# Attention scores: the second product of each block made over 128 rows instead of 68

## The chip, the cores and the metric

The kernel runs on one core of one Trainium2 chip. A core has TensorE (PE: matrix products; PEld is its loading of weights), VectorE (DVE), ScalarE (ACT), GpSimd (POOL) and SyncE (SP, which here issues most transfers). The metric is the device time of one execution in microseconds (us). [...]

## What is computed

Attention with a causal mask and a bias that falls with the distance, then a layer of eight experts of which each row takes one, then a mixing layer. Only the first part is touched:

```python
scores = scale * np.matmul(q, k.transpose(0, 1, 3, 2))        # 4 x 8 heads, 576 x 576, head size 64
cum = np.cumsum(np.maximum(s, 0.0), axis=-1)
bias = -(cum[:, :, :, None] - cum[:, :, None, :])
scores = np.where(causal, -1e9, scores + np.minimum(bias, 0.0))
attn = np.exp(scores - max); attn = attn / (attn.sum() + 1e-9)
out = np.matmul(attn, v)
# then the experts (w_gate, w_local, w1, w2) and the mixing layer (U, V, w_ch1, w_ch2)
```

## The kernel before

The program is written out by hand for each engine: `ORDER` (lines 29 to 127) is a list of numbers that says in which order the pieces of the attention, of the router and of the first expert's work are issued, and each engine works through its own list in that order.

The 32 heads are taken in 16 pairs. For each pair the kernel builds a stack `OP` of 128 rows (two buffers, used in turn, line 416). Its columns are four blocks of 576: K1, Q1, K2, Q2. Each of q and k is split into a high and a low part, so that a product of the two is a sum of three products. The first 64 rows of K1 and Q1, and the last 64, together hold two of them, and the **first product** (lines 725 to 731) contracts all 128 rows of Q1 with K1. K2 and Q2 hold the third in rows 0 to 63, and in rows 64 to 67 the two parts of the bias (cumulated sums against ones), so the **second product** (lines 732 to 738) contracts rows 0 to 67 (`SK = D + 4`) and adds to the same place. Rows 68 to 127 of K2 and Q2 aren't used. In a block on the diagonal a third, small product with a 128x128 mask follows (line 740).

A pair has five blocks of rows (`t` = 0 to 4), each with two parts; so there are 16 x 6 x 2 = 192 first and 192 second products, with 64 to 448 columns. After a block's products DVE takes the largest of each row (line 749), ACT the exponentials (line 766), PE turns them (line 795), ACT and DVE split them (lines 803 and 808), and PE multiplies them with v (line 844).

The stack is filled by transfers on SP's queue: `bias(n)` writes rows 64 to 67 of K2 and Q2 (lines 461 to 465) and `stack` copies the parts (line 557). For the first pair ACT, DVE and POOL write the parts themselves (`split_twice`, lines 1299 to 1318), POOL the block Q2 (line 1304). Of the setup code the prediction speaks of the reading of `s` and its cumulated sum on DVE (lines 424 to 437), and of the loads of `v` that POOL issues (line 1323).

## Time and profile before

| | us |
|---|---|
| runs, median of 3 | 997.5 (996.58 to 1003.1) |
| the profiled execution, its own time | 1002.29 |
| its span, from the first instruction to the last | 1000.6 |
| PE busy in the span | 946.6 |
| DVE, ACT, POOL busy | 550.6, 455.1, 235.2 |

The span is what the profile shows; the time of the same execution is 1.7 us more. Attention and routing take about the first 300 us, the experts and the mixing layer the rest. The mean granted clock over the span is 0.969.

### The profile page before, as it was taken

Reading aid. Unit: us, or ns where it says so; the run is one execution under the profiler, and the core shown is the slowest. Engines: PE = TensorE matmul, PEld = TensorE weight load, DVE = VectorE, ACT = ScalarE, POOL = GpSimd, SP = SyncE. Lnnn points to the kernel's source line nnn. Section 1 sums busy time; section 2 is a strip of 40 time slices with the busy share of each in tenths; the row PEclk is TensorE's granted clock in tenths of the full one; section 3 lists DMA queues with packets and bytes.
Section 4 is the critical chain, followed back from the end, with each engine's and each line's share of the span. In section 5 each row is a group of like instructions: output and inputs, shape, how many; then the busy total and the mean of one; then the engine's idle time right before and its main releaser. Section 6 shows DMA issues by size and latency. Waiting matters only on the chain.

```text
span 1000.6 us, 17314 instructions
## 1 busy us (share of the span) xinstructions
PE 946.6 (95%) x6378; PEld 727.8 (73%) x6378; DVE 550.6 (55%) x1168; ACT 455.1 (45%) x1040; POOL 235.2 (24%) x355
## 2 busy tenths in 40 slices
PE   5888988989899899999999999999999999999997
PEld 4777987978786588887878866666666666666676
DVE  6776884685675478777777847862123212212121
ACT  4766875675662457546647653342122112112111
POOL 6634325123353233234144312220000000000000
PEclk9998997797989999999999999999999999999999
DMA  6977888588702678667655733312000200100010
GB/s 175 216 165 171 185 205 187 118 222 181 216 23 84 222 230 250 192 215 215 187 160 173 237 130 117 115 43 84 1 1 0 84 1 1 64 1 1 1 43 22
DMA packets 130816, 123.45 MB, mean 123 GB/s; under 512 B 57280, under 2 KB 102656, under 8 KB 128928
## 3 DMA queue, kind: packets, MB, share of 16 engines
q1 hardware_dynamic: 124224, 109.04, 40.4%
q0 software_dynamic: 5296, 12.89, 4.1%
q8 instruction: 53, 0.87, 0.4%
q10 hardware_dynamic: 1200, 0.30, 0.1%
q14 instruction: 43, 0.35, 0.1%
HBM read 81.04 MB, written 16.33 MB: 97 GB/s over the span
## 4 chain that ended last, share of the span: by engine, by line
PE 58%; DVE 2%; issue 2%; DMA 1%; ACT 1%; POOL 1%; SPq 0%; DVEq 0%; POOLq 0%
PE acc L1913 28%; PE ps_h L1899 26%; DMA yt_d<-y,idx 1%; PE pu L2178 1%; PE ups L2384 1%; PE xps L1653 1%; DVE w2u L247 1%; PE ph L2341 0%; POOL w2u L247 0%; ACT y L1668 0%; PE acc_b L2298 0%; DMA ut<-yt_d 0%; PE ps_b L2287 0%; DVE t L293 0%; DVE hl L1872 0%
## 5 line engine op out<-in xcount | busy, mean ns | idle before, releaser
L1872 DVE SCALAR_TENSOR_TENSOR hl<-ps_h,hh 128x512 fp32r<-128x512 f32 (+6 forms) x136 | 78.0, 574 | 251.3 <-ACT hh L1871 249.9
L1871 ACT ACTIVATE hh<-ps_h 128x512 fp32r<-128x512 f32 (+6 forms) x136 | 68.7, 505 | 308.8 <-PE ps_h L1899 308.8
L1899 PE MATMUL ps_h<-ux,c1u 128*128 128x512 f16 (+1 forms) x960 | 199.9, 358 | 0.5 <-DVE ux L2387 0.5
L1913 PE MATMUL acc<-w2u,hh 128*128 128x512 f32 (+4 forms) x592 | 192.2, 406 | 0.0
L1899 PEld LDWEIGHTS <-c1u 128*128 128x128 f16 x960 | 88.3, 98 | 98.3 <-issue 20.1
L1913 PEld LDWEIGHTS acc<-w2u,hh 128*128 128x128 f32 (+4 forms) x592 | 106.0, 184 | 25.4
L1913 PE MATMUL acc<-w2u,hl 128*128 128x512 f32 (+4 forms) x296 | 116.7, 394 | 0.0
L1899 PE MATMUL ps_h<-xh,w1u 128*128 128x256 f32 (+5 forms) x448 | 108.0, 314 | 3.4 <-DVE hl L1872 3.1
L808 DVE SCALAR_TENSOR_TENSOR lo<-pp,hi 128x384 f16<-128x384 f32 (+2 forms) x160 | 85.9, 550 | 24.9 <-ACT hi L803 24.0
L1913 PE MATMUL acc<-c2u,hh 128*128 128x512 f32 x288 | 95.6, 413 | 0.0
L803 ACT ACTIVATE hi<-pp 128x384 f16<-128x384 f32 (+2 forms) x160 | 77.5, 496 | 29.5 <-PE pp L795 27.5
L795 PE MATMUL pp<-ident,Pb 128*128 128x128 f32 x480 | 85.9, 303 | 2.9 <-DVE parts L499 1.7
L766 ACT ACTIVATE Pb<-sp,nm 128x192 f32<-128x192 f32 (+4 forms) x160 | 81.0, 538 | 5.2 <-DVE nm L749 4.1
L1899 PEld LDWEIGHTS ps_h<-xh,w1u 128*128 128x128 f32 x448 | 76.9, 188 | 8.2 <-DVE hl L1872 4.3
L725 PE MATMUL sp<-OP 128*128 128x288 f32 (+4 forms) x192 | 74.3, 391 | 8.6 <-DMA OP<-parts 4.5
L749 DVE TENSOR_REDUCE nm<-sp 128x1 f32<-128x576 f32 (+4 forms) x96 | 67.7, 705 | 18.7 <-PE sp L740 18.3
L1899 PE MATMUL ps_h<-xl,w1u 128*128 128x256 f32 (+5 forms) x224 | 68.9, 308 | 0.0
L732 PE MATMUL sp<-OP 68*128 68x288 f32 (+4 forms) x192 | 63.2, 333 | 1.6 <-DMA OP<-b_d 1.6
L1913 PEld LDWEIGHTS acc<-w2u,hl 128*128 128x128 f32 (+4 forms) x296 | 54.2, 183 | 14.2
L1913 PEld LDWEIGHTS acc<-c2u,hh 128*128 128x128 f32 x288 | 53.5, 188 | 13.4
L844 PE MATMUL ob<-VP,hi 128*128 128x65 f16 x960 | 59.0, 199 | 4.2 <-ACT xr L856 4.2
L795 PEld LDWEIGHTS pp<-ident,Pb 128*128 128x128 f32 x480 | 58.2, 156 | 4.7 <-DVE parts L499 2.4
(287 smaller groups left out, 1637.4 us busy)
## 6 DMA issues: line engine op xcount, KB each, us to landing
raw<-in_moe_w_ch_dram SPq DMA_DIRECT2D x32, 512.0 KB
OP<-parts SPq DMA_DIRECT2D x28, 576.0 KB
raw_in<-in_moe_w_dram SPq DMA_DIRECT2D x56, 256.0 KB
raw_out<-in_moe_w_dram SPq DMA_DIRECT2D x56, 256.0 KB
OP<-parts SPq DMA_DIRECT2D x28, 288.0 KB
kn<-in_k_dram SPq DMA_DIRECT2D x32, 128.0 KB
x_d<-x SPq DMA_DIRECT2D x16, 256.0 KB
raw_a<-in_moe_w_dram SPq DMA_DIRECT2D x16, 256.0 KB
```

What stands on the lines that cost most here:

```text
L725: nc.tensor.matmul(sp[:, c, :cw], lhsT=W1[j][:, h, t * P : (t + 1) * P], rhs=K1[j][:, h, c0 : c0 + cw], start=True, stop=False,)
L732: nc.tensor.matmul(sp[:, c, :cw], lhsT=W2[j][0:SK, h, t * P : (t + 1) * P], rhs=K2[j][0:SK, h, c0 : c0 + cw], start=False, stop=not diag,)
L749: nc.vector.tensor_reduce(out=k["nm"] if two else k["nm"][:, 0:1], in_=k["sp"], op=ALU.min, axis=AX.X if two else AX.XY,)
L766: nc.scalar.activation(out_, in_, AF.Exp, scale=-1.0, bias=k["nm"][:, x : x + 1])
L795: nc.tensor.transpose(pp[:, i - i0], k["pb"][:, a, x * P : (x + 1) * P], ident)
L803: nc.scalar.activation(k["hi"][:, i0:i1], k["pp", i0][:, : i1 - i0], AF.Copy, scale=SCALE)
L808: nc.vector.scalar_tensor_tensor(out=k["lo"][:, i0:i1], in0=k["pp", i0][:, : i1 - i0], scalar=SCALE, in1=k["hi"][:, i0:i1], op0=ALU.mult, ...
L844: nc.tensor.matmul(o[:, h], lhsT=pt[:, a * (t + 1) + x], rhs=VP[n % 2][:, z, x, h], start=(x == 0 and i == 0), stop=(x == t and i == len(t ...
L1871: nc.scalar.activation(hh[:, :n], ps[:, :n], AF.Relu)
L1872: nc.vector.scalar_tensor_tensor(out=hl[:, :n], in0=ps[:, :n], scalar=0.0, in1=hh[:, :n].bitcast(F32), op0=ALU.max, op1=ALU.subtract,)
L1899: nc.tensor.matmul(ps[:, x * cut : (x + 1) * cut], lhsT=wa[:, kk], rhs=xa[:, kk, :cut], start=(kk == 0 and i == 0), stop=(kk == KD - 1 and ...
L1913: nc.tensor.matmul(acc[i][0:m], lhsT=ha[:, sl], rhs=u2[g][:, wa], start=(g == 0 and jj == 0), stop=(g == nf - 1 and jj == 2),)
```

## The change

The second product takes all 128 rows of K2 and Q2. Rows 68 to 127 have to hold zero in both buffers, so each of them is cleared once at the start: the first by DVE, ahead of its first other work, the second by POOL, behind the loads of `v` that it issues. The rows 64 to 67 that the clearing also covers are written by the bias afterwards.

```diff
-        SK = D + 4
@@
         OP = [ap.tile([P, 2, 4 * S], F32R, name=f"OP{i}") for i in range(NB)]
+        nc.vector.memset(OP[0][D:P, :, 2 * S :].bitcast(F32), 0.0)
@@
                     nc.tensor.matmul(
                         sp[:, c, :cw],
-                        lhsT=W2[j][0:SK, h, t * P : (t + 1) * P],
-                        rhs=K2[j][0:SK, h, c0 : c0 + cw],
+                        lhsT=W2[j][:, h, t * P : (t + 1) * P],
+                        rhs=K2[j][:, h, c0 : c0 + cw],
                         start=False,
                         stop=not diag,
                     )
@@
         ld_heads(v, vn[0][:, :, 0:2], 0, 0, 2, nc.gpsimd)
+        nc.gpsimd.memset(OP[1][D:P, :, 2 * S :].bitcast(F32), 0.0)
```

On PE, ACT and SP the instructions and their order stay as they were. DVE's list begins so before the change (`Pb` holds `s` and its sums):

```order
L2551 UNCONDITIONAL_BRANCH
L424 TENSOR_SCALAR Pb_121<-Pb_121 32x576
L427 SCALAR_TENSOR_TENSOR Pb_121<-Pb_121 32x576
L430 CAST OP_134<-Pb_121 32x576
L431 COPY Pb_122<-OP_134 32x576
```

and so with it (`OP_133` is the first buffer of the stack):

```order
L2552 UNCONDITIONAL_BRANCH
L416 MEMSET OP_133 64x2x1152
L424 TENSOR_SCALAR Pb_121<-Pb_121 32x576
L427 SCALAR_TENSOR_TENSOR Pb_121<-Pb_121 32x576
L430 CAST OP_134<-Pb_121 32x576
```

The clearing stands ahead of the chain that makes the cumulated sums. POOL's list, from the setup's last clearing to the copies of Q2 for the first pair, before the change:

```order
L581 MEMSET ones 1x128
L386 DMA vn_119<-in_v_dram 64x2x64
L390 DMA vn_119<-in_v_dram 128x4x64 x2
L1304 CAST OP_133<-OP_133 64x448
L1304 CAST OP_133<-OP_133 64x128
```

and with it (`OP_134` is the second buffer):

```order
L581 MEMSET ones 1x128
L385 DMA vn_119<-in_v_dram 64x2x64
L389 DMA vn_119<-in_v_dram 128x4x64 x2
L1324 MEMSET OP_134 64x2x1152
L1304 CAST OP_133<-OP_133 64x448
L1304 CAST OP_133<-OP_133 64x128
```

The clearing stands between the loads and the copies.

## Rows read from the trace of the kernel before

**Rows 1.** The span in two stretches: busy time of each engine, count, clock.

```profile
core 0: us, PE busy (x) PEld busy (x) DVE busy (x) ACT busy (x) POOL busy (x), PEclk, DMA share, GB/s
0.00:300.00 300.00, 261.07 (x2912) 232.26 (x2913) 210.02 (x512) 202.38 (x529) 121.58 (x222) 0.90 0.74 172
300.00:1000.60 700.60, 685.50 (x3468) 495.52 (x3467) 340.62 (x657) 252.67 (x512) 113.60 (x133) 1.00 0.33 103
```

**Rows 2.** The same columns, around the three long stretches at the lower clock.

```profile
163.10:187.00 23.90, 23.74 (x156) 22.54 (x157) 10.44 (x30) 11.50 (x27) 5.16 (x7) 0.50 0.62 138
187.00:238.20 51.20, 45.32 (x596) 39.46 (x594) 41.14 (x102) 39.83 (x106) 14.71 (x21) 1.00 0.80 189
238.20:248.50 10.30, 10.30 (x62) 9.59 (x61) 5.19 (x16) 4.35 (x11) 4.01 (x5) 0.50 0.75 158
248.50:272.30 23.80, 20.34 (x259) 17.76 (x259) 16.43 (x34) 16.87 (x46) 10.73 (x16) 1.00 0.88 235
272.30:282.60 10.30, 9.92 (x66) 8.72 (x66) 6.78 (x14) 5.03 (x15) 3.31 (x3) 0.50 0.06 20
282.60:300.00 17.40, 15.24 (x225) 13.78 (x224) 12.90 (x32) 11.78 (x29) 9.99 (x13) 1.00 0.12 32
```

**Rows 3.** The same columns, the first and the fourth of five short stretches.

```profile
26.60:30.00 3.40, 3.40 (x17) 3.26 (x18) 1.94 (x5) 1.43 (x5) 3.06 (x4) 0.50 0.96 211
94.90:98.30 3.40, 3.40 (x34) 3.34 (x30) 2.31 (x8) 1.82 (x4) 1.60 (x2) 0.50 0.66 130
```

**Rows 4.** PE in order of time: the idle time ahead of the long stretches, with its releaser.

```profile
start us, us, engine line op out<-in xcount [idle before <-releaser]
163.26 1.45 PE L1031 MATMUL sm<-wg,xT 128*128 128x9 f32 x6 [3.92 <-DVE parts L499]
...
238.03 0.33 PE L487 MATMUL pt<-ident,kn 128*128 128x128 f32 x1 [1.93 <-DVE parts L499]
...
270.72 0.35 PE L725 MATMUL sp<-OP 128*128 128x192 f32 x1 [2.04 <-DMA OP<-parts]
272.68 0.53 PE L732 MATMUL sp<-OP 68*128 68x192 f32 x1 [1.60 <-DMA OP<-b_d]
```

**Rows 5.** Groups by shape: the widest common form of both products (busy us, mean ns).

```profile
L725 PE MATMUL sp<-OP 128*128 128x288 f32 x64 | 23.8, 382 | 4.2 <-DMA OP<-parts 2.5 <-DMA OP<-ring 1.1 <-DVE OP L1311 0.5
L732 PE MATMUL sp<-OP 68*128 68x288 f32 x64 | 20.9, 338 | 0.0
L725 PEld LDWEIGHTS sp<-OP 128*128 128x128 f32 x192 | 42.3, 220 | 10.9 <-ACT Pb L766 3.6 <-issue 3.3 <-DMA OP<-parts 2.3
L732 PEld LDWEIGHTS sp<-OP 68*128 68x128 f32 x192 | 41.8, 218 | 1.9 <-DMA OP<-b_d 1.9
```

**Rows 6.** PE in order of time: one block of scores at the higher clock.

```profile
101.78 0.38 PE L725 MATMUL sp<-OP 128*128 128x288 f32 x1
102.00 0.30 PE L732 MATMUL sp<-OP 68*128 68x288 f32 x1
102.14 0.30 PE L725 MATMUL sp<-OP 128*128 128x288 f32 x1
102.27 0.30 PE L732 MATMUL sp<-OP 68*128 68x288 f32 x1
102.41 0.23 PE L740 MATMUL sp<-maskb,identb 128*128 128x128 bf16 x1
```

**Rows 7.** The second products alone (line 732): PE busy and count in low stretches.

```profile
core 0: us, PE busy (x) PEld busy (x), PEclk, DMA share, GB/s
163.10:187.00 23.90, 4.34 (x10) 3.32 (x10) 0.50 0.62 138
238.20:245.00 6.80, 1.77 (x4) 1.32 (x4) 0.50 0.62 124
245.00:248.50 3.50, 0.00 (x0) 0.00 (x0) 0.51 0.99 223
272.30:282.60 10.30, 3.39 (x8) 2.62 (x8) 0.50 0.06 20
57.30:60.70 3.40, 1.45 (x3) 0.76 (x3) 0.50 0.83 188
94.90:98.30 3.40, 0.00 (x0) 0.00 (x0) 0.50 0.66 130
```

**Rows 8.** The start, in order of time: DVE, then POOL, then PE.

```profile
2.70 0.45 DVE L424 TENSOR_SCALAR Pb<-Pb 32x576 f32<-32x576 f32 x1 [2.70 <-DMA Pb<-in_s_dram]
6.22 0.75 DVE L435 TENSOR_SCALAR Pb<-Pb 32x1152 f32<-32x1152 f32 x1
7.70 0.62 DVE L1305 TENSOR_TENSOR OP<-pt,OP 64x448 fp32r<-64x448 f32 x1
...
4.02 0.30 POOL L567 MEMSET vn<- 64x256 f32 x1
6.00 2.02 POOL L390 DMA_DIRECT2D vn<-in_v_dram  x2
9.45 0.79 POOL L1304 CAST OP<-OP 64x448 fp32r<-64x448 f32 x2 [1.42 <-ACT OP L1303]
...
12.94 0.44 PE L732 MATMUL sp<-OP 68*128 68x288 f32 x1
```

## The prediction

> **What bounds the kernel now.** I read first the busy time and the clock in two stretches, then the pieces in which the clock is low, then the two products by shape and in order of time, then the start.

> PE is busy for 261.07 of the first 300 us and 685.50 of the other 700.6, more than any other engine [rows 1]. All second products lie in the first stretch, and only there does the granted clock fall: 0.90 on average, against 1.00 behind it. So the change can act only on attention, and there PE is what the others wait for most of the time, apart from some stalls.

> The lower clock comes in eight stretches: five short ones of 3.4 us each (17 us together, the first and the fourth in [rows 3]), and three long ones of 23.90, 10.30 and 10.30 us, 44.5 us together [rows 2]. Each long one follows a wait of PE: 3.92 us for DVE's parts, 1.93 us for the same, and 2.04 and 1.60 us for transfers into the stack [rows 4]. The reader is to see the price of the low level in the counts of [rows 2]: at 0.50 PE did 156 + 62 + 66 = 284 products in 44.5 us, 6.38 per us; at 1.00, in the pieces between them, 596 + 259 + 225 = 1080 in 92.4 us, 11.69 per us. (The mix is much the same: the pairs repeat.) So the work of 44.5 us would have taken 284 / 11.69 = 24.3 us: the long stretches cost 20.2 us, and each us at the low level costs 0.454 us.

> **The change, part by part.**

> *The products themselves: nothing.* A second product of 288 columns has a mean of 338 ns, a first one 382 ns [rows 5]. That difference is not the rows: the busy time of a matmul begins before its weights are there, and the first of a block waits for them. In an undisturbed block [rows 6] second products over 68 rows and the first product over 128 that follows stand 0.14 us apart, first and second 0.13, and all three show 0.30 us. The weight loads take 220 and 218 ns [rows 5]. So 192 products over 60 rows more add 0. If the difference of the means were due to the rows, it would be 44 ns x 192 = 8.4 us; that is the upper bound.

> *The two clearings: 0.2 us, once.* Neither engine shows one of 64 x 2304. On DVE the nearest rows are a pass over 1152 elements in 0.75 us and one over 448 with two inputs in 0.62 us [rows 8], so by size 1.5 to 3.2 us. DVE has been idle until 2.70, when `s` lands, and the clearing needs no input, so it lies in that gap for the most part. What remains, 0 to 0.6 us, delays the chain of the sums, and behind it the bias, which SP transfers, and the second product of the first block. On POOL a clearing of 64 x 256 took 0.30 us, so 64 x 2304 takes 2.7 us by size. It starts at 8.02, when the loads are issued, and the copy of Q2 moves from 9.45 to about 10.7, its end from 10.24 to 11.5. It is still ahead of the first second product at 12.94, which waits for it, so it costs nothing; without that cover of 1.4 us it would cost 1.3 us. Bounds for both: 0 to 1.9 us; I take 0.2, since both gaps are in the rows.

> *The clock: the only term that can matter.* The second products are the one common kind of matmul here that uses about half the rows of the array. If what the chip counts as PE's work goes by the rows in use, a product over 128 rows counts for more than one over 68, and after a stall the clock comes back sooner. What the rows say: the modelled busy time does not separate stretches that end soon from stretches that last. PE was busy for 3.40 of 3.40 us in the short ones, and the clock rose; it was busy for 23.74 of 23.90 in the long one, and it stayed low [rows 2, 3]. So something other than being occupied counts. The second products have 4.34 us of that long stretch, 10 of them, and 3.39 us of the one at 272; in the stretch at 238 there are four in the 6.8 us that stayed low and none in the last 3.5 us, after which the clock rose; in the short one at 94.9 there are none either [rows 7]. That fits. But the short stretch at 57.3 has three and rose all the same [rows 7], so this is support, not proof.

> [...]

> Bounds of the term. Below: the long stretches stay, 0 us. Above: each shrinks to the length of a short one, 44.5 - 3 x 3.4 = 34.3 us less, worth 34.3 x 0.454 = 15.6 us. The falls themselves stay, since they follow waits in which PE does nothing [rows 4]. I take half, 7.8 us, since the second products are only part of what PE does there (4.34 of 23.74 us, 3.39 of 9.92).

> *The sum.* Against the profiled execution: 1002.3 - 7.8 + 0.2 = 994.7 us. But that execution lies 4.8 us above 997.5, the median of the runs shown. If the scatter is the low clock too, a median run has 4.8 / 0.454 = 10.6 us less of it: 23.7 of the 34.3 us are left, half of which is worth 5.4 us. So for the median **997.5 - 5.4 + 0.2 = 992.3 us**. With all of it gone both ways of counting give 986.9.

> **The rivals.**

> *The clock does not go by rows.* Then PE is as busy in the low stretches as before, since no product lasts longer (23.74 of 23.90, 10.30 of 10.30 us leave no room), the clock comes back when it did, and 997.5 + 0.2 = 997.7 us result, somewhere between 996.6 and 1003 as the runs scatter. For it: the stretch at 57.3 that rose with three second products in it. Against it: the equal busy shares above.

> *The rows cost time* (the other side). If PE takes longer over 128 rows, by 44 ns each as the means of [rows 5] have it, 8.4 us are added in a stretch that PE bounds: 997.5 + 8.4 + 0.2 = 1006.1 us; from 53 ns each (10.2 us) the kernel would be slower by over 1%. Against it: the equal distances in [rows 6]. It decides if those distances grow.

> *The start grows.* DVE's clearing ends later than the landing of `s`, or POOL's holds the copy beyond 12.94: at most 1.9 us, 999.4 us.

> **How the numbers follow.** The clock returns earlier: 0.5, with 992.3 us and a range of its own from 986.9 (all of it) to 997.7 (nothing). No effect of rows: 0.4. Rows cost time: 0.05. The start grows: 0.05. The range for 8 in 10 goes from 986 to 1002 us: below, to the bound of the recovered clock and 1 us of scatter; above, to the scatter of a kernel that has not changed; the slower rival is left out. About 1% is what a measurement of this kernel can tell from no change, since its runs differ by 0.65% already. Faster by over 1% means below 987.5 us: the part of the first case in which nearly all of the long stretches go, about a third of it, 0.17. Slower by over 1% means above 1007.5: most of the slower rival and a mishap at the start, 0.05. Within 1%: 0.78.

> **What would show it.** In the changed kernel's profile: the distance between the products of a block at 288 columns stays at 0.13 to 0.14 us (or the second rival is right). The copy of Q2 on POOL ends before the first second product, and that starts within 0.6 us of 12.94. The first 300 us show the same number of falls of the clock, but the long stretches are shorter, so that the mean clock rises from 0.90 and attention ends earlier by 0.454 us for each us. If the stretches at 0.50 add up to 60 us or more as now, the term of the clock was wrong, and the time is that of the first rival. If they shrink and the time does not, the gain was lost behind attention.

## The result, and the profile after

The changed kernel takes 995.28 us (median of 20 runs, 986.86 to 1004.11), and the kernel before 1003.18 us (20 runs, the three earlier ones among them, 995.99 to 1009.9). The ratio is 0.9911, with an interval of 0.9886 to 0.9936. Against 997.5 us, the median of the three earlier runs, 992.3 had been forecast.

The kernel before itself differs from one comparison to the next (its medians were 1003.18, 998.24, 997.86 and 999.0 us), so the changed kernel was timed twice more, each time beside it: 0.9976 [0.9943, 1.001] and 0.993 [0.9902, 0.9957]. The ratios leave out runs over 1.5% above the fastest of the same kernel, while all means below are over every run of a set; so the two need not agree in the last digit. Over the three comparisons and the one of the experiments the mean is 998.91 us before (101 runs) and 993.26 us changed (44 runs): 5.65 us less, about 0.6%.

The profiled execution took 995.22 us with a span of 993.5 us (before: 1002.29 and 1000.6), and its mean granted clock over the span is 0.977 (before: 0.969). The granted clock is TensorE's, as the profile gives it; in the traces of both kernels it is 1.00 or 0.50 in every stretch on record, and any other figure is a mean. The two stretches of [rows 1], in the changed kernel; the columns are the stretch in us, its length, the busy time (count) of PE, PEld, DVE, ACT and POOL, the granted clock, the DMA share and GB/s:

```profile
core 0: us, PE busy (x) PEld busy (x) DVE busy (x) ACT busy (x) POOL busy (x), PEclk, DMA share, GB/s
0.00:300.00 300.00, 256.92 (x2999) 227.92 (x2999) 216.71 (x533) 206.62 (x539) 124.72 (x225) 0.93 0.76 176
300.00:993.50 693.50, 678.57 (x3382) 489.56 (x3381) 335.45 (x637) 248.20 (x501) 115.01 (x131) 1.00 0.32 102
```

The difference is in the first row: the clock is 0.93 instead of 0.90, and in the same 300 us PE gets through 2999 products instead of 2912. What is ahead then is 7.1 us at the end of the span.

The pieces at 0.50, by the same view and columns (six of ten; of the four left out each is 3.4 to 3.5 us long):

```profile
25.80:32.70 6.90, 6.65 (x53) 6.10 (x54) 3.93 (x12) 3.67 (x9) 4.97 (x8) 0.51 0.96 203
...
165.80:172.60 6.80, 6.30 (x33) 5.81 (x34) 4.00 (x11) 3.85 (x10) 4.44 (x6) 0.50 0.48 101
217.00:220.40 3.40, 3.16 (x19) 2.90 (x20) 2.71 (x8) 2.59 (x8) 1.04 (x1) 0.50 0.75 219
247.70:251.10 3.40, 3.40 (x23) 2.26 (x21) 2.52 (x7) 2.32 (x8) 1.48 (x3) 0.50 1.01 297
264.80:271.60 6.80, 4.95 (x38) 4.67 (x38) 3.42 (x7) 1.98 (x7) 1.75 (x1) 0.50 0.28 75
329.60:333.00 3.40, 2.77 (x10) 1.72 (x8) 2.18 (x4) 1.25 (x3) 0.75 (x2) 0.50 0.81 286
```

The falls are still there: nine in the first 300 us, where there were eight, and one behind them. But none lasts longer than 6.9 us. All ten together are 44.4 us, against 61.5 (44.5 + 17) before.

Where do they stand? PE of the changed kernel in order of time (start, length, what, idle time before with its releaser), to be read beside [rows 4]:

```profile
166.29 1.45 PE L1031 MATMUL sm<-wg,xT 128*128 128x9 f32 x6 [4.14 <-DVE parts L499]
...
217.24 1.12 PE L487 MATMUL pt<-ident,qn 128*128 128x128 f32 x4 [2.25 <-DVE parts L499]
...
233.91 0.33 PE L487 MATMUL pt<-ident,kn 128*128 128x128 f32 x1 [1.54 <-DVE parts L499]
...
264.56 0.38 PE L725 MATMUL sp<-OP 128*128 128x192 f32 x1 [2.07 <-DMA OP<-parts]
266.79 0.53 PE L732 MATMUL sp<-OP 128*128 128x192 f32 x1 [1.85 <-DMA OP<-b_d]
```

And of the kernel before, one wait that [rows 4] leave out:

```profile
222.02 0.66 PE L487 MATMUL pt<-ident,qn 128*128 128x128 f32 x4 [1.91 <-DVE parts L499]
```

Two of the three long stretches have come down at the same place, behind waits as long as before: 23.90 to 6.80 us (wait 3.92 us, now 4.14) and 10.30 to 6.80 us (2.04 and 1.60 us, now 2.07 and 1.85). The other has no counterpart. The wait ahead of it (1.93 us, at 238.03) is now 1.54 us at 233.91, and no fall follows. The fall at 217.00 is new: its wait stood at 222.02 before, 1.91 us long, and the clock stayed at 1.00 there (187.00 to 238.20 in [rows 2]). So in this pair of executions the stretches are shorter, and the falls are in part others.

One pair is not enough to call that shown. The kernel with the clearings alone (below) has its second product over 68 rows as before, and its profiled execution took 989.92 us: eight stretches, 37.5 us at 0.50 in all, one of them long. The profiled execution of the changed kernel's first repeat has a long one too. The first row is of the former, the second of the latter:

```profile
58.40:68.60 10.20, 9.89 (x73) 8.64 (x73) 6.13 (x18) 6.65 (x18) 0.97 (x4) 0.50 0.49 111
57.40:67.60 10.20, 9.27 (x70) 8.07 (x70) 5.63 (x16) 6.04 (x16) 0.36 (x2) 0.50 0.43 96
```

Of seven traces without small products (below), the two over 68 rows have four stretches of 10 us or more, and the five over 96 or 128 rows have one. Single executions scatter; the effect has to be read from means over runs.

### The profile page after: what moved, and what is told of

Read it like the earlier page. It is cut to its first block, busy times and chain, and to the rows that moved or that the text cites. A ratio compares the mean times of both kernels' runs of the same rounds, so it can differ in the third digit from the quotient of the medians.

```text
span 993.5 us, 17318 instructions
## 1 busy us (share of the span) xinstructions
PE 935.5 (94%) x6378; PEld 717.5 (72%) x6378; DVE 552.2 (56%) x1169; ACT 454.8 (46%) x1040; POOL 239.7 (24%) x356
## 4 chain that ended last, share of the span: by engine, by line
PE 79%; DMA 7%; DVE 5%; ACT 3%; SPq 3%; issue 2%; POOL 0%; POOLq 0%; ACTq 0%; DVEq 0%
PE acc L1914 29%; PE ps_h L1900 27%; PE pp L795 4%; DMA OP<-parts 3%; PE ob L844 3%; PE sp L725 2%; PE sp L732 2%; PE sm L1031 1%; SPq L557 1%; PE pu L2179 1%; PE pt L487 1%; PE xtp L1018 1%; PE xps L1654 1%; PE ups L2385 1%; PE sp L740 1%
## 5 line engine op out<-in xcount | busy, mean ns | idle before, releaser
L795 PE MATMUL pp<-ident,Pb 128*128 128x128 f32 x480 | 82.2, 293 | 2.6 <-DVE parts L499 1.5
L725 PE MATMUL sp<-OP 128*128 128x288 f32 (+4 forms) x192 | 72.0, 380 | 9.6 <-DMA OP<-parts 4.9
L732 PE MATMUL sp<-OP 128*128 128x288 f32 (+4 forms) x192 | 61.0, 322 | 1.9 <-DMA OP<-b_d 1.9
L844 PEld LDWEIGHTS <-hi 128*128 128x128 f16 x960 | 54.7, 102 | 7.7 <-issue 5.5
```

The lines of the kernel that those rows point to most:

```text
L725: nc.tensor.matmul(sp[:, c, :cw], lhsT=W1[j][:, h, t * P : (t + 1) * P], rhs=K1[j][:, h, c0 : c0 + cw], start=True, stop=False,)
L732: nc.tensor.matmul(sp[:, c, :cw], lhsT=W2[j][:, h, t * P : (t + 1) * P], rhs=K2[j][:, h, c0 : c0 + cw], start=False, stop=not diag,)
L795: nc.tensor.transpose(pp[:, i - i0], k["pb"][:, a, x * P : (x + 1) * P], ident)
L844: nc.tensor.matmul(o[:, h], lhsT=pt[:, a * (t + 1) + x], rhs=VP[n % 2][:, z, x, h], start=(x == 0 and i == 0), stop=(x == t and i == len(t ...
```

## The experiments

Ten more programs were run; two of them are the changed kernel again. Each short diff is against the changed kernel. A mean time is given with its standard error over the runs of that set, and beside it the mean "low time": the time at the lower clock, which is 2 x (1 - mean granted clock) x span of each run, since the traces of both kernels show no clock other than 1.00 and 0.50.

### Only the clearings; 96 rows; ones instead of zeros

The first undoes the products and keeps both clearings:

```diff
-                        lhsT=W2[j][:, h, t * P : (t + 1) * P],
-                        rhs=K2[j][:, h, c0 : c0 + cw],
+                        lhsT=W2[j][0 : D + 4, h, t * P : (t + 1) * P],
+                        rhs=K2[j][0 : D + 4, h, c0 : c0 + cw],
```

> The two clearings of the changed kernel, but the second product over 68 rows as before. If the gain comes from the rows of the product (my theory), nothing of it is left: 1.000 times the kernel before, within 0.4%, and the long stretches at the lower clock are as before (some 60 us at 0.50 in the span). If the gain comes from the clearings or from a start that is shifted against the clock, this kernel is as fast as the changed one, about 0.991 times the kernel before.

The second has `0:96` in the same two places.

> The second product over 96 rows, of which 28 are zero. If the clock goes by the rows in use, the gain is part of that over 128 rows (28 of 60 rows): 0.994 to 0.998 times the kernel before. If it goes by whether all rows are used, there is no gain: 1.000. If it goes by something that any added row brings, 0.991.

The third takes all 128 rows, and the added rows of K2 hold ones instead of zeros (those of Q2 stay zero, so the sum is the same):

```diff
-        nc.vector.memset(OP[0][D:P, :, 2 * S :].bitcast(F32), 0.0)
+        nc.vector.memset(OP[0][D:P, :, 2 * S : 3 * S].bitcast(F32), 1.0)
+        nc.vector.memset(OP[0][D:P, :, 3 * S :].bitcast(F32), 0.0)
@@ and the same for OP[1] on gpsimd
```

> All 128 rows as in the changed kernel, but the added rows of K2 (the operand that streams) hold ones instead of zeros, those of Q2 (the weights) zeros; the sum is the same. If the number of rows counts, as in the changed kernel: 0.991 times the kernel before, within 0.4%. If moving values count too, the clock comes back sooner still: 0.985 to 0.988, mean clock above 0.980.

Measured, on one chip (12 runs each, 29 of the kernel before):

| kernel | ratio to before | mean us | low time, us |
|---|---|---|---|
| before | | 998.05 ± 0.76 | 61.8 ± 2.3 |
| clearings only, 68 rows | 0.9996 [0.9962, 1.0031] | 997.04 ± 1.23 | 53.6 ± 3.0 |
| 96 rows | 0.9959 [0.9922, 0.9996] | 993.45 ± 1.21 | 46.5 ± 2.9 |
| 128 rows, ones | 0.9959 [0.9928, 0.9991] | 991.27 ± 0.74 | 42.2 ± 1.8 |

The first and the third row below "before" differ by the rows alone (and the ones), and by 5.8 us; their low time differs by 11.4 us, which at the 0.454 us of the prediction is worth 5.2 us. The standard error of the 5.8 us is 1.4, that of the 11.4 us 3.5. Between 68 and 96 rows it is 3.6 us of time (error 1.7) against 7.1 us of low time (error 4.2), worth 3.2 us. So the gain belongs to the products, not to the clearings, and it goes with the low time. Whether 96 rows give less than 128 is not settled: the intervals overlap. The 96 rows came out within what was expected (0.994 to 0.998); the ones missed theirs by a little (0.9959 against 0.987 to 0.995; 0.993 by the means), and nothing speaks for moving values counting too, which was to give 0.985 to 0.988.

A miss remains. The low time of the clearings-only kernel lies 8.2 us below that of the kernel before, though its products are the same, and its time only 1.0 us. About 60 us had been expected. Both differences are about two standard errors or less, so I take them for scatter, but that is not shown.

The price of the clearings can be read in this kernel too. DVE and PE at its start, in order of time:

```profile
1.37 1.98 DVE L416 MEMSET OP<- 64x2304 f32 x1 [1.37 <-PEq L2537]
3.38 0.59 DVE L424 TENSOR_SCALAR Pb<-Pb 32x576 f32<-32x576 f32 x1
```

```profile
13.34 0.59 PE L725 MATMUL sp<-OP 128*128 128x288 f32 x1
13.72 0.44 PE L732 MATMUL sp<-OP 68*128 68x288 f32 x1
13.96 0.44 PE L725 MATMUL sp<-OP 128*128 128x288 f32 x1
14.20 0.44 PE L732 MATMUL sp<-OP 68*128 68x288 f32 x1
```

The first second product starts at 13.72, against 12.94 before [rows 8], over 68 rows. The clock is on record in this trace only from 20.8 us on. But products over 68 and over 128 rows stand 0.24 us apart here, both ways, which is the distance of equal products at 0.50 in the next section.

### Equal products after a pause

Here the whole computation is left out. PE waits some 7 us, then does equal products of 288 columns one behind the other, over 128, 68, 64 and 32 rows in turn, each time after such a pause; then the same with 96 and 64 columns.

```python
for rows, n, count in PHASES:      # (128, 288, 120), (68, 288, 120), (64, 288, 120), ...
    ...                            # DVE is busy some 7 us, then writes x, for which PE waits
    for i in range(count):
        nc.tensor.matmul(o[:, 0:n], lhsT=w[i % 2][0:rows], rhs=x[0:rows, 0:n],
                         start=True, stop=True)
```

> Measures the disputed thing by itself: the whole computation is left out. PE idles for about 11 us, then makes a row of equal products, 12 times: 288, 96 and 64 columns, each over 128, 68, 64 and 32 rows (120 products of 288 columns, 200 of the others). If the clock goes by the rows in use, the granted clock rises in the stretches over 128 rows and later or not at all in those over 32, at 288 columns and above all at 96. If it goes by how busy PE is, the four stretches of one width look the same. If rows cost time, the products over 128 rows stand further apart than those over 32 at the same clock; my theory says equal.

Measured, the first four stretches (128, 68, 64 and 32 rows), with the columns of [rows 1]. In the first, the clock is on record only from 17.3 us on, so its 1.00 holds for the later part:

```profile
11.10:29.80 18.70, 18.67 (x120) 18.63 (x120) 0.00 (x0) 0.00 (x0) 1.00 0.29 106
37.50:66.40 28.90, 28.90 (x120) 28.77 (x120) 0.00 (x0) 0.00 (x0) 0.50 0.00 1
74.10:103.00 28.90, 28.90 (x120) 28.78 (x120) 0.00 (x0) 0.00 (x0) 0.50 0.00 1
110.70:139.60 28.90, 28.90 (x120) 28.80 (x120) 0.00 (x0) 0.00 (x0) 0.50 0.00 1
```

This is the clearest result of all. Over 128 rows the clock is at 1.00 by 17.3 us at the latest, and 120 products take 18.70 us. Over 68, 64 and 32 rows PE is occupied for 28.90 of 28.90 us, and the clock stays at 0.50 all that time. At 0.50 a product took the same time over each of these numbers of rows: 28.90 / 120 = 0.241 us over 68, 64 and 32; over 128 rows, 18 of them in 4.40 us at 0.50 in the next run are 0.244 us. With 96 and 64 columns the clock stayed at 0.50 for all four numbers of rows, 128 too (200 products kept PE busy for 42.9 us in each of these stretches, and a mean clock of 0.532 over the 542.2 us of the run leaves some 35 us for 1.00, of which the first stretch has all up to 29.80), so those stretches tell nothing of rows; but they show that rows were not all that counted. The one over 128 rows and 96 columns:

```profile
147.30:190.00 42.70, 42.69 (x200) 42.69 (x200) 0.00 (x0) 0.00 (x0) 0.50 0.00 0
```

The stretch over 128 rows is also the first of the run, behind a pause of 11.13 us and not 7.46. In the next run the stretches that rise stand before and behind one that doesn't, each after 7.46 us, so the longer pause does not explain it.

### Which rows, which values, which mixture

In the same manner (the whole computation left out), 288 columns, nine stretches: 128, 112, 96 and 80 rows; 128 rows of which 64 are zero in both operands, then in the weights only; 128 and 68 rows in turn; 128 rows and 128 rows with zeros in turn; and 60 products over 128 rows followed without a pause by 120 over 68.

```python
PHASES = [([(128, 0, 0)], 120), ([(112, 0, 0)], 120), ([(96, 0, 0)], 120), ([(80, 0, 0)], 120),
    ([(128, 1, 1)], 120), ([(128, 1, 0)], 120),          # rows, zero weights, zero data
    ([(128, 0, 0), (68, 0, 0)], 160), ([(128, 0, 0), (128, 1, 1)], 160),
    ([(128, 0, 0)] * 60 + [(68, 0, 0)] * 120, 180)]
```

> The whole computation is left out; as in the first such run, PE idles for about 11 us and then makes a row of products of 288 columns, nine times: over 128, 112, 96 and 80 rows; over 128 rows with the lower 64 zero in both operands, then in the weights alone; 128 and 68 rows in turn; 128 and 128 with zeros in turn; 60 over 128 rows and behind them 120 over 68. If rows count and not values, the two stretches with zeros rise as the first does, the alternation of 128 and 68 later or not at all, and that of 128 and 128 with zeros as the first. If values count, those with zeros rise later. Whether 112 and 96 rise tells how much of the rows it takes here. Behind the 60 products over 128 rows the clock falls, if what was high needs the rows to stay, or stays, if busy is enough for that.

Measured, from the second stretch on, in that order and with the same columns. The alternation of 128 and 68 rows and the one with zeros stand twice, whole and up to the rise of the clock. The last stretch is cut at the rise and where the products over 68 rows begin:

```profile
37.90:55.40 17.50, 17.50 (x120) 17.39 (x120) 0.99 (x2) 0.00 (x0) 0.90 0.00 1
63.00:81.50 18.50, 18.50 (x120) 18.40 (x120) 1.01 (x2) 0.00 (x0) 0.85 0.00 1
89.10:118.00 28.90, 28.90 (x120) 28.82 (x120) 1.03 (x2) 0.00 (x0) 0.50 0.00 1
127.00:144.40 17.40, 17.40 (x120) 17.23 (x120) 0.00 (x0) 0.00 (x0) 0.91 0.00 1
151.90:170.40 18.50, 18.47 (x120) 18.33 (x120) 1.06 (x2) 0.00 (x0) 0.85 0.00 0
178.00:202.50 24.50, 24.50 (x160) 24.35 (x160) 0.98 (x2) 0.00 (x0) 0.86 0.01 1
178.00:184.70 6.70, 6.70 (x28) 6.70 (x29) 0.98 (x2) 0.00 (x0) 0.50 0.01 2
210.00:234.30 24.30, 23.62 (x160) 23.16 (x160) 1.07 (x2) 0.00 (x0) 0.89 0.00 1
210.00:215.50 5.50, 4.82 (x18) 4.50 (x19) 1.07 (x2) 0.00 (x0) 0.50 0.00 0
241.80:246.20 4.40, 4.35 (x18) 4.36 (x19) 1.08 (x2) 0.00 (x0) 0.50 0.00 0
246.20:251.70 5.50, 5.50 (x44) 5.50 (x43) 0.00 (x0) 0.00 (x0) 1.00 0.00 0
251.70:267.70 16.00, 16.00 (x123) 15.85 (x121) 0.00 (x0) 0.00 (x0) 1.00 0.00 1
```

Four things were measured. Over 112 and 96 rows the clock rose (120 products in 17.50 and 18.50 us, mean clock 0.90 and 0.85), over 80 it didn't (28.90 us at 0.50). What the rows held made no difference: with half of them zero, the clock rose as soon as without (17.40 and 18.50 us for 120 products, as over 112 and 96 rows). The number of rows mattered for the rise and not for staying: once the clock was high, products over 68 rows kept it at 1.00 for the 16.00 us that they lasted. And one thing speaks against a simple story: 128 and 68 rows in turn rose too, 6.7 us after their start. That is the latest of all the rises (5.5 us for 128 and 128 in turn, 3.2 to 5.7 us in the others), but it is a single stretch, and 160 products took 24.50 us against 24.30. So the alternation of products over 128 and 68 rows alone held the clock down for 6.7 us and no longer; the kernel's mixture around its waits, with other products and short pauses between, must make the difference. That last step is argued, not shown.

### Small products that keep PE at work

If the low time is what costs, one can try to prevent the falls. At twelve places of the changed kernel where PE idles, small products that nobody reads (a 128x128 one with 126 columns, into an unused part of `ob`) are put ahead of the waiting one, 264 in all (the expectation below counts 244):

```diff
+FILL = {329: 14, 389: 30, 594: 32, 756: 24, ...}    # place in PE's list: how many
+        nc.tensor.fill = lambda pe: pe.matmul(
+            ob[:, 386:512], lhsT=identb, rhs=maskb[:, 0:126], start=True, stop=True
+        )
```

The changed kernel was run once more beside it, and the same small products in the kernel before.

> The changed kernel once more, on the chip of the runs beside it. 0.991 to 0.996 times the kernel before; some 43 us at the lower clock in a run, against 62 of the kernel before; the time at equal mean clock the same as that of the kernel before. If the gain were more than the clock, it would be faster at equal clock too.

> The changed kernel with 14 to 32 small products (128 rows, 126 columns, into unused columns of ob) put ahead of each of the twelve instructions before which PE idles for over 1.3 us in every trace, so that PE works where it waited. If the falls of the clock come from those waits, most falls go: fewer than 15 us at 0.50, 0.985 times the changed kernel or 0.978 times the kernel before. If the small products wait for others or delay what follows (244 of them, at some 55 ns 13 us in all), the gain is eaten: 0.995 to 1.005 times the kernel before.

> The same small products in the kernel before, with its second product over 68 rows. If the rows matter only for how fast the clock comes back, then without falls they hardly matter: within 0.4% of the changed kernel with the small products. If a stretch of attention over 68 rows falls by itself, it stays 0.5 to 1% slower than that one.

Measured, on one chip (12 runs each, 29 of the kernel before):

| kernel | ratio to before | mean us | low time, us |
|---|---|---|---|
| before | | 997.19 ± 0.81 | 55.6 ± 1.9 |
| changed | 0.9976 [0.9943, 1.001] | 993.32 ± 0.86 | 46.8 ± 1.9 |
| changed, small products | 0.9995 [0.9959, 1.003] | 996.88 ± 1.22 | 26.6 ± 2.9 |
| before, small products | 0.9982 [0.9946, 1.0018] | 997.52 ± 1.71 | 29.4 ± 4.0 |

The repeat of the changed kernel missed what was expected (0.991 to 0.996; 0.9976, or 0.996 by the means). The small products do in part what they were put there for: 20.2 us less low time than in the changed kernel, worth 9.2 us, though not the fewer than 15 us that had been expected. The time is 3.6 us longer all the same, so at this price they cost some 13 us. One reason stands in PE's list in order of time (changed kernel with small products):

```profile
78.49 3.15 PE L609 MATMUL ob<-maskb,identb 128*128 128x126 bf16 x32 [2.66 <-ACT xr L888]
```

At five of the places they waited themselves, here for ACT, which still read `ob`, and ran behind the wait instead of inside it (32 in 3.15 us, 98 ns each, where some 55 had been expected). The lower two rows of the table differ by the rows of the second product, and by 0.6 us with errors of 1.2 and 1.7: where the falls are kept away by other means, no effect of the rows is left to be seen. That fits the clock. But the error of the difference is 2.1 us and the gain on this chip is 3.9, so these two rows alone don't exclude a gain by another way.

A last attempt left out the places that waited, and where a new tile of scores came next it put the small products into that tile (172 products at eight places):

> The changed kernel with small products only at eight of the places, those where the run with all of them showed that they ran inside PE's wait, or where they can go into the scores' own tile, so that they wait for nobody else; 12 to 36 each. If the cost of the run with all of them lay in the places at which the small products had to wait for ScalarE, the time at equal mean clock is now that of the changed kernel, and with about 10 us less at the lower clock it is 0.993 to 0.997 times the changed kernel. If PE's work there costs time wherever it is put, no gain: 1.000 to 1.005 times the changed kernel.

> The changed kernel once more, beside the kernel with small products on the same chip, to get the size of the gain from more runs: 0.991 to 0.998 times the kernel before, with 43 to 47 us at the lower clock.

On one chip (12 runs each) the ratio to the kernel before was 0.9926 [0.9889, 0.9963] with them and 0.993 [0.9902, 0.9957] for the changed kernel alone; the means are 990.63 ± 1.12 and 991.23 ± 0.86 us, the low times 29.5 and 43.2 us. The 13.7 us of low time that it saves are worth 6.2 us; 0.6 us are left, no gain that can be measured, where 0.993 to 0.997 times the changed kernel had been expected. PE of that kernel, in order of time:

```profile
205.59 1.59 PE L612 MATMUL ob<-maskb,identb 128*128 128x126 bf16 x26
211.53 0.69 PE L148 MATMUL pt<-ident,qn 128*128 128x128 f32 x2 [4.35 <-DVE parts L528]
```

At this place they run ahead of the wait (26 in 1.59 us, 61 ns each) and are done 4.35 us before it ends. At another (92.15 us) they still waited themselves, 1.59 us, for ACT. So nothing that was tried is shown to be faster than the changed kernel.

## Why the prediction was right, and where it was not

**Products cost nothing: right.** A block of the changed kernel at the high clock, to be set against [rows 6], and the two groups by shape in the first 300 us:

```profile
104.74 0.38 PE L725 MATMUL sp<-OP 128*128 128x288 f32 x1
104.95 0.30 PE L732 MATMUL sp<-OP 128*128 128x288 f32 x1
105.09 0.30 PE L725 MATMUL sp<-OP 128*128 128x288 f32 x1
105.22 0.30 PE L732 MATMUL sp<-OP 128*128 128x288 f32 x1
```

```profile
L725 PE MATMUL sp<-OP 128*128 128x288 f32 x64 | 23.0, 372 | 4.8 <-DMA OP<-parts 2.8 <-DMA OP<-ring 1.5 <-DVE OP L1311 0.5
L732 PE MATMUL sp<-OP 128*128 128x288 f32 x64 | 20.0, 324 | 0.0
```

The distances are 0.13 to 0.14 us as before. In both, the first product of the block is busy for 0.38 us and the three behind it for 0.30. Its weights, in the block of [rows 6], come with a load of their own just ahead:

```profile
101.76 0.19 PEld L725 LDWEIGHTS sp<-OP 128*128 128x128 f32 x1
```

That product counts as busy from 101.78, 0.17 us before its load ends; the other three start 0.05 to 0.06 us before theirs end. Second products now have as many rows as first ones, and their means still differ by 48 ns (372 and 324; 382 and 338 in [rows 5]). So that difference was never the rows, as the prediction had it, and the rival that the rows cost time has fallen.

**The clearings: mis-sized.** The prediction took 0.2 us, from "DVE has been idle until 2.70, when `s` lands". The start of the changed kernel, DVE, POOL and PE in order of time:

```profile
1.36 1.98 DVE L416 MEMSET OP<- 64x2304 f32 x1 [1.36 <-PEq L2537]
3.38 0.58 DVE L424 TENSOR_SCALAR Pb<-Pb 32x576 f32<-32x576 f32 x1
```

```profile
8.10 2.14 POOL L1324 MEMSET OP<- 64x2304 f32 x1
10.30 0.79 POOL L1304 CAST OP<-OP 64x448 fp32r<-64x448 f32 x2
```

```profile
13.71 0.44 PE L732 MATMUL sp<-OP 128*128 128x288 f32 x1
```

The clearing's length, 1.98 us, lies within the 1.5 to 3.2 us that had been worked out. What was missed is that DVE's list itself begins only at 1.36 us, so the gap was 1.34 us wide and not 2.7. DVE's chain starts 0.68 us later (3.38 against 2.70), and the first second product 0.77 us later (13.71 against 12.94): outside the 0.6 us that the prediction allowed, within its bounds of 0 to 1.9. On POOL the step held: the copies of Q2 end at 11.09, well ahead of 13.71, and cost nothing.

**The clock: right in direction; the size was in part luck.** That the clock rose over some numbers of rows and not over others is shown by the equal products (at 288 columns over 128, 112 and 96, not over 80, 68, 64 and 32), and that the changed products bring less low time by the means (42.2 against 53.6 us for ones and clearings only). That the stretches in the kernel end sooner, as the prediction has it, is seen in the profiled pair and not shown beyond it: a mean clock does not tell shorter stretches from fewer falls. One premise did not hold as it stood, "the falls themselves stay": of the three long stretches one is gone, and another fall has come.

In the profiled pair the low time went from 61.5 to 44.4 us. These 17.1 us x 0.454 are 7.8 us, half of the 34.3 us that could go, as forecast; less 0.77 at the start that is 7.0, and the span is 7.1 us shorter. That it is the half so closely is luck: the half was a choice between nothing and all, and the profiled execution with the clearings alone, over 68 rows, had less low time (37.5 us) than the changed kernel's.

Over the two repeats and the runs of the kernel before on the three chips of the experiments, the low time is 58.9 us before and 45.0 changed: 13.9 x 0.454 - 0.77 = 5.5 us, against a measured 5.6 (997.92 against 992.28, with an error of about 0.8). Over all four, 5.65 us were measured, against 5.2 forecast for the median (5.4 - 0.2). The first comparison alone came to 8.4 us in its mean and was the largest of the three (3.9 and 7.4 in the repeats); since the kernel before was slowest there, the forecast of 992.3 from 997.5 is better judged by the four together.

The price of 0.454 us is borne out by the 20 runs of the changed kernel: a line through their times against their low time rises by 0.45 us for each us. In the later runs it is flatter: 0.31 for the 81 of the kernel before, 0.36 for the 24 repeats of the changed one. At 0.36 the sum would be 13.9 x 0.36 - 0.77 = 4.2 us, and 1.4 of the 5.6 us, near two errors, would have no account. It may be that some of the low time falls where PE is not waited for; that is not shown. Nor does any run show by itself that the 0.77 us at the start reach the end.

**The mean clock above 0.90, attention ending earlier: right** (0.93). "The same number of falls" was nearly right (nine for eight, and one at 329.6 in the experts' part). One reading was too round: of the five short stretches before, PE was busy for 3.40 of 3.40 us in four, and for 2.96 in the one at 77.80.

**The first rival, that the clock does not go by rows: fallen,** by the equal products: 28.90 us of unbroken work over 68 rows without a rise, and a rise over 128 by 17.3 us at the latest. Had busy time alone decided, the four stretches would have risen alike. They did not: here the rows in use counted for the rise. No run shows a clock that goes by busy time alone, which this rival's 997.7 us took for granted.

What stays open: why the alternating products rose although the kernel's low stretches, before, lasted up to 23.9 us; and why the low time of the kernel before differs between comparisons (55.6 to 61.8 us in the sets above). No run took the waits away, and none tells whether the falls in the kernel end sooner or are fewer.

## What to carry to other kernels

A product over few rows took no less time here than one over all 128 (0.241 us over 32, 64 and 68 rows, 0.244 over 128, at 0.50), and behind a wait of PE of 7.46 us a row of such products left the clock at 0.50 (28.90 us over 68 rows). Where rows of the operands are free, filling them with zeros once can be tried: here it cost a clearing at the start (0.77 us later at the first second product) and nothing on PE (distances of 0.13 to 0.14 us as before), and was worth about 0.6%. Look for this where the profile shows stretches at 0.50 that last far longer than the wait ahead of them, and judge the worth by their length times what one such us costs, not by the products. Take that length from many runs, not from one trace. A clearing "in a gap" was hidden here only from the moment at which the engine's list began to run (1.36 us on DVE), so read that moment first.
